# A windowed attention and two gated layers on one core: another order of the first loads, a fourth place for raw weights and for an attention unit, and filler products ahead of the first real one

## Chip, core and metric

The kernel runs on one core of a Trainium2 chip. The metric is the device time of one execution in microseconds (us). Three runs of the kernel before gave 659.75, 659.79 and 660.41 us, median 659.79.

## What is computed

```python
# attention, q, k, v: [2, 8, 768, 64]; a key is kept if it is one of the first 8 or at most 95 positions back
scores = scale * q @ k.T + bias(head, distance);  a = softmax(where(keep, scores, -1e9));  x = a @ v
x = x.transpose(0, 2, 1, 3).reshape(1536, 512)
y = ((x @ w_a) * (x @ w_b)) @ w_out            # d_ff 1536
h = y @ w_in                                   # d_ff 2048
g = where(h >= 1, h, where(h <= -1, 0, (h + 1)**2 / 4));  out = g @ w_out2
```

The weights come in double precision: the kernel gets each as 64 raw bits and makes two float32 halves (high and low) of it on the chip. Each of the large products is then three products: high by high, high by low and low by high.

## The kernel before

The 1536 rows are three tiles of 512. There are 24 **attention units** (tile, pair of heads, 256 rows). A unit's steps are: **scores** (S, L681 to L699), a minimum over the row with the mask added (VectorE, L711), the exponential with its sum (ScalarE, L723), an addition to the four sums (ScalarE, L731), a reciprocal (VectorE, L734), four **norms** (VectorE or GpSimd, L750), two **turns** (T, transposes on TensorE, L758, and their copies out of PSUM on ScalarE or VectorE, L764), and **values** (V, L775). The values' result is split into the two halves of x (L656, L657). In the first tile units alternate between a first block of rows (three 128-wide places, so T has 3+3 transposes and V is short) and a full one (4+4).

The **products** (p below, L459 and L487, the first four groups in L609) are 2460 matmuls of 128x512 in a fixed order; the first needs tile 0's first x and the first unit of weights. A unit of **weights** is 512 KB of raw bits (tile `raw`), loaded by `load_raw` into one of `NRAW` places and turned into two halves by seven steps (`prep`, L363 to L398: ScalarE L391, VectorE L392 to L395, a copy L402/L404, a subtraction L397). There are 68 such units.

All loads go out on SyncE's queue (SP). `Loads.begin` (L281) writes out the first ones before the branch on the flag; later ones are issued as places come free. The program uses eight load counters in turn, so each load also waits until the load eight before it has landed.

The order of everything after the branch is written by a planner at build time (`Clock`, L108): it keeps a model clock, sends an operation to the engine that would end it first by the durations given in the code, and advances by a given time for each step on TensorE. In the main loop (L995) it takes an attention step if one is due, or if the next product cannot start; otherwise a product. The chip then runs each engine's list in that fixed order, with waits on semaphores. So a wrong duration costs nothing by itself: it puts an operation at a place in an engine's list where it stands and waits while others behind it could go.

Of the kernel before, what the change touches and what calls it, by code (L numbers as in the profile page):

```python
# [10 lines left out]
F32 = mybir.dt.float32  # L11
F32R = mybir.dt.float32r
BF16 = mybir.dt.bfloat16
# [29 lines left out]

NRAW = 3

WARM = 10

TINY, HUGE = 3.0517578125e-05, 122880.0
# [10 lines left out]
HOP = dict(tensor=200, scalar=160, vector=170, gpsimd=120)  # L59
DMA = dict(issue=475, begin=1125, rate=360, end=900)  # L60

BEFORE = 4450

# [134 lines left out]
class Loads:  # L198
# [82 lines left out]
    def begin(self):  # L281
        self.load(0)
        self.load_raw(0)
        self.load(1)
        self.load_raw(1)
        self.load_v(0)
        self.load_raw(2)
        self.load(2)
        for n in range(3, NRAW):
            self.load_raw(n)  # L290
        self.load_v(1)

# [8 lines left out]
class Ffn:  # L301
    NW, MORE = 12, 2
    NM, MORE_M = 5, 4

    def __init__(self, ctx, tc, clock, loads, out, half):
        self.tc, self.nc, self.clock, self.loads, self.out, self.half = tc, tc.nc, clock, loads, out, half
        pool = lambda name, bufs, **kw: ctx.enter_context(tc.tile_pool(name=name, bufs=bufs, **kw))
        self.slots = []
        self.more_slots(ctx, "w_hl", self.NW)
        self.p_bits = pool("w_bits", 2)  # L310
        self.p_x = pool("x_hl", NP * NT)
        self.p_part = pool("part", NP * NT)
        self.mids = []
        self.more_mids(ctx, "mid", self.NM)
        self.p_s = pool("scr", 2)
        self.ps_acc = pool("ps_acc", 2, space=PSUM)
        self.ps_ab = pool("ps_ab", 2, space=PSUM)
        self.todo, units = plan()
        self.unit_no = {u: n for n, u in enumerate(units)}
        self.n_units = len(units)  # L320
        self.first_use, self.last_use = {}, {}
        for n, item in enumerate(self.todo):
            for u in units_of(item):
                self.first_use.setdefault(self.unit_no[u], n)
# [7 lines left out]
        self.in_flight = 0  # L332
        self.gap = GAP["first"]
        self.room = dict(ab=2, acc=2, s1=2, s2=2)
        clock.poll = self.prepare
# [27 lines left out]
    def prep(self, urgent):  # L363
# [11 lines left out]
        def chain(*steps):  # L375
            (emit, costs), rest = steps[0], steps[1:]

            def then():
                if len(rest) == 2:
                    self.loads.load_raw(u + NRAW, clock)  # L380
                if rest:
                    chain(*rest)
                else:
                    self.w[u] = wh, wl
                    self.in_flight -= 1

            clock.on(slack, emit, then, **costs)
# [200 lines left out]
    def early(self):  # L588
        nc = self.nc
        pools = [(self.ps_ab, "ab")] * 2 + [(self.ps_acc, "acc")] * 2  # L590
        pools = pools[: 2 * EARLY]
        early_ps = []
        for pool, tag in pools:
            self.take(tag)
            early_ps.append(pool.tile([P, T], F32, tag=tag, name=f"e{len(early_ps)}"))
        for c in range(NP):
            for n in range(2 * EARLY):
# [3 lines left out]
                yield lambda: u in self.w and (kind, t, c) in self.ready  # L601
                wh, wl = (a[:, c * P : (c + 1) * P] for a in self.w[u])
                xh, xl = self.x[0][c]
                ps = early_ps[n]
# [19 lines left out]
class Attention:  # L624
# [20 lines left out]
    def to_x(self, ps, t, p, col, w):  # L645
# [11 lines left out]
        lo = lambda e: e.tensor_tensor(places[1], ps[:, :w], as_f32(places[0]), ALU.subtract)  # L657
        low = lambda: clock.on(SLACK["x"], lo, then, None, False, vector=315)
        clock.on(SLACK["x"], hi, low, None, False, scalar=264, vector=315)


class Window(Attention):
# [4 lines left out]

    UNITS = 3

# [11 lines left out]
    def scores(self, st):  # L681
# [15 lines left out]
        w0, w1 = (w for _, w in places)  # L697
        ns = (w0 + w1) * 5 // 3 + w1 * 5 // 6 + 200
        self.write(ns, lambda: [self.reduce(st, j, r, ps[j]) for j in range(2) for r in range(NQ)])  # L699

    def reduce(self, st, j, r, ps):
# [14 lines left out]
        def reduced():  # L716
            st["read", j] = st.get(("read", j), 0) + 1
            if st["read", j] == NQ:
                self.give(ps)
            clock.on(SLACK["exp"], exp, share, scalar=100 + w * 25 // 16)  # L720

# [3 lines left out]
        def share():  # L725
            st["exp"] = st.get("exp", 0) + 1
            if st["exp"] == 2 * NQ:
                clock.on(SLACK["share"], add, lambda: clock.on(SLACK["share"], inverse, norms, None, False, vector=85), scalar=200)

# [6 lines left out]
        def norms():  # L736
            for jj in range(2):
                for rr in range(NQ):
                    clock.on(SLACK["norm"], *self.norm(st, jj, rr), gpsimd=457, vector=202)

        clock.on(SLACK["reduce"], least, reduced, lambda: not i or not self.masks.left, False, vector=w * 4 // 3)

# [9 lines left out]
    def turn(self, st, j):  # L752
# [11 lines left out]
        copy = lambda e: self.ffn.copy(e, pt[:, :n], ps[:, :n])  # L764
        self.write(n * 110 // P, lambda: clock.on(SLACK["turn"], copy, out, None, False, scalar=52 + n * 5 // 6, vector=n * 7 // 6))

    def values(self, st):

        ps, v = self.take(), st["v"]
        for r, (at, w) in enumerate(self.places(st)):  # L770
            parts = (0, 1) if w == self.W else (1,)
            for n, x in enumerate(parts):
                for j in range(2):
# [4 lines left out]
                    )  # L778
        ns = 1076 if st["i0"] else 807
        self.write(ns, lambda: self.to_x(ps, st["t_no"], st["p"], st["col"], NQ * P))  # L780

    def steps(self):
# [6 lines left out]
        def score(n):  # L789
            self.scores(units[n])  # L790
            loads.load(n + 3, self.clock)
            if n + 1 < len(units):
                nxt = units[n + 1]
                here = lambda: nxt.update(qs=True)
                scale = lambda e: loads.scale(e, n + 1, self.scales)
                self.clock.on(SLACK["qk"], scale, here, lambda: "here" in nxt, gpsimd=430, vector=200)

# [25 lines left out]
class Dense(Attention):  # L823


    def __init__(self, ctx, early, tc, clock, ffn, args, ident, ng, nl):
        super().__init__(ctx, tc, clock, ffn, ident)
        self.qz, self.k2, self.qd, self.kd, self.vd = args
        self.ng, self.nl = ng, nl
# [25 lines left out]
    def block(self, t, m):  # L855
# [5 lines left out]
        for p in range(NP):  # L861
            name = f"{b}_{i}_{p}"
            q = pool.tile([P, 2, P], F32, tag="q", name="q" + name)
# [3 lines left out]
            v = pool.tile([P, NB, 2 * D], F32, tag="v", name="v" + name)  # L867
            nc.sync.dma_start(v, self.vd[b, p, :, :, 1])
            nc.vector.tensor_scalar_mul(q, q, D**-0.5)
            po = self.ffn.ps_acc.tile([P, T], F32, tag="acc", name="o" + name)  # L870
            for j in range(2):
# [33 lines left out]
                for kb in range(NB):  # L905
                    nc.tensor.matmul(
                        po[row, :P], v[:, kb, row], st_[:, kb * P : (kb + 1) * P],
                        start=kb == 0, stop=kb == NB - 1,
# [15 lines left out]
def tile_kernel(ctx: ExitStack, tc: tile.TileContext, nn, qz, k2, qd, kd, vd, wu, out):  # L924
# [54 lines left out]
    with tc.If(near != 0, preferred_fallthrough_block=True) as cmp:  # L979
        with ExitStack() as arm:  # L980
# [14 lines left out]
            while holds:  # L995
# [8 lines left out]
                elif holds():  # L1004
                    passed += 1
                    holds = next(products, None)
                    if ffn.now == starts[2] and early:
# [3 lines left out]
                        ffn.more_mids(arm, "mid_more", ffn.MORE_M)  # L1011
                        ffn.gap = GAP["later"]
                else:
                    clock.turn()
            clock.drain()
    with cmp.Else():
        with ExitStack() as arm:
# [4 lines left out]
            early = arm.enter_context(ExitStack())  # L1022
            Dense(arm, early, tc, clock, ffn, (qz, k2, qd, kd, vd), ident, ng, nl).run()
            early.close()
# [110 lines left out]
```

## Time and profile before

| | |
|---|---|
| median of three runs | 659.79 us |
| the profiled execution | 660.28 us, span 658.5 us |
| TensorE (PE) busy | 643.0 us (98%), 3190 matmuls |
| VectorE (DVE) busy | 476.5 us (72%) |
| ScalarE (ACT) busy | 234.8 us (36%) |
| GpSimd (POOL) busy | 28.3 us (4%) |
| mean granted clock of PE | 0.991 of full |

Busy time of PE overlaps the tail of one matmul with the next, so that a busy PE may still be slower than it can be: single matmuls spread out read as busy. What one step costs when nothing holds it back is read from the chain of waits, where steps stand end to end.

### The profile page before, as it was taken

The page shows a single profiled execution, that of the slowest core. Times are in us where ns is not written, and L with a number is a line of the kernel's source. Part 1 is how long each engine was busy: PE and PEld are TensorE (multiplying, and loading weights), DVE is VectorE, ACT ScalarE, POOL GpSimd, SP SyncE. Part 2 cuts the span into 40 slices and gives each one's busy share as a digit, 9 for nine tenths or more (in the row PEclk, how much of TensorE's full clock was granted, in tenths as well). Part 3 has the DMA queues.
Part 4 walks back from the last instruction along what each step waited for, and adds up shares of the span by engine and source line. Part 5 has one row for each costly group of instructions (what it writes and reads, how often), then busy time and mean ns, then how long its engine had stood idle before and what let it go on. Part 6 is the DMA issues. An engine that isn't in the chain of part 4 may idle for free.

```text
span 658.5 us, 8812 instructions
## 1 busy us (share of the span) xinstructions
PE 643.0 (98%) x3190; PEld 514.4 (78%) x3190; DVE 476.5 (72%) x1071; ACT 234.8 (36%) x528; POOL 28.3 (4%) x64
## 2 busy tenths in 40 slices
PE   5999999999999999999999999999999999999997
PEld 2666677778888888888888888888888888888886
DVE  6999998537782837953848988785789688755552
ACT  4777775534241212311312323453334233311110
POOL 2223310000000000000000000000000000000000
PEclk7999999999999999999999999999999999999999
DMA  7666555101340211420212320321122111000112
GB/s 217 178 198 194 162 146 165 34 1 64 100 156 1 67 61 47 140 70 1 72 56 64 108 85 5 123 85 44 48 82 81 48 61 36 0 1 17 48 49 85
DMA packets 23763, 52.69 MB, mean 80 GB/s; under 512 B 3104, under 2 KB 11552, under 8 KB 23712
## 3 DMA queue, kind: packets, MB, share of 16 engines
q1 hardware_dynamic: 23568, 52.05, 25.4%
q8 instruction: 27, 0.44, 0.3%
q14 instruction: 24, 0.20, 0.1%
q10 hardware_dynamic: 144, 0.00, 0.0%
HBM read 48.89 MB, written 3.15 MB: 79 GB/s over the span
## 4 chain that ended last, share of the span: by engine, by line
PE 90%; DVE 5%; DMA 3%; SPq 1%; issue 1%; ACT 0%; DVEq 0%
PE ps L459 48%; PE o L487 20%; PE y L487 15%; PE at L775 2%; PE at L694 2%; PE at L758 2%; DVE p L711 1%; DMA v<-in_vd 1%; DMA k<-in_k 1%; DVE p L750 1%; PE e L609 1%; SPq L275 1%; DMA raw<-in_wu 1%; DVE bits L395 1%; DVE xlx L657 0%
## 5 line engine op out<-in xcount | busy, mean ns | idle before, releaser
L459 PE MATMUL ps<-xhx,w_hlh 128*128 128x512 f32 x224 | 88.7, 396 | 0.0
L459 PE MATMUL ps<-xlx,w_hlh 128*128 128x512 f32 x224 | 88.2, 394 | 0.0
L459 PE MATMUL ps<-xhx,w_hll 128*128 128x512 f32 x224 | 87.9, 392 | 0.0
L535 ACT ACTIVATE c<-c,half 128x512 f32<-128x512 f32 x48 | 34.7, 723 | 135.7 <-DVE c L532 135.7
L518 DVE TENSOR_TENSOR ab<-ps,a 128x512 f32<-128x512 f32 x34 | 23.4, 688 | 61.7 <-PE ps L459 61.4
L459 PE MATMUL ps<-xhy,w_hlh 128*128 128x512 f32 x168 | 65.4, 389 | 0.0
L459 PE MATMUL ps<-xly,w_hlh 128*128 128x512 f32 x168 | 65.4, 389 | 0.0
L459 PE MATMUL ps<-xhy,w_hll 128*128 128x512 f32 x168 | 65.4, 389 | 0.0
L532 DVE TENSOR_SCALAR c<-ps 128x512 f32<-128x512 f32 x48 | 33.1, 690 | 39.5 <-PE ps L459 39.4
L540 DVE TENSOR_TENSOR g<-ps,c 128x512 f32<-128x512 f32 x48 | 33.1, 690 | 24.2 <-ACT c L535 23.8
L402 ACT COPY a<-ps 128x512 f32<-128x512 f32 x28 | 16.4, 587 | 95.5 <-PE ps L459 91.7
L459 PEld LDWEIGHTS ps<-xhx,w_hlh 128*128 128x128 f32 x224 | 42.1, 188 | 9.3 <-issue 1.4
L391 ACT ACTIVATE bits<-raw 128x512 f32<-128x512 f32 x68 | 44.5, 667 | 13.4 <-DVE w_hll L397 6.1
L459 PEld LDWEIGHTS ps<-xlx,w_hlh 128*128 128x128 f32 x224 | 42.1, 188 | 9.2 <-issue 1.2
L459 PEld LDWEIGHTS ps<-xhx,w_hll 128*128 128x128 f32 x224 | 42.1, 188 | 9.0 <-issue 0.7
L395 DVE SCALAR_TENSOR_TENSOR bits<-raw,bits 128x512 uint32<-128x512 uint32 x68 | 46.4, 689 | 0.5
L394 DVE SCALAR_TENSOR_TENSOR bits<-raw,bits 128x512 uint32<-128x512 uint32 x68 | 46.1, 686 | 0.3
L402 ACT CAST w_hlh<-bits 128x512 fp32r<-128x512 f32 x46 | 28.4, 620 | 48.0 <-DVE bits L395 47.9
L397 DVE TENSOR_TENSOR w_hll<-bits,w_hlh 128x512 fp32r<-128x512 f32 x54 | 36.9, 685 | 1.7
L487 PE MATMUL y<-midh,w_hll 128*128 128x512 f32 x96 | 37.9, 394 | 0.0
L487 PE MATMUL y<-midh,w_hlh 128*128 128x512 f32 x96 | 37.8, 394 | 0.0
L487 PE MATMUL y<-midl,w_hlh 128*128 128x512 f32 x96 | 37.7, 392 | 0.0
(296 smaller groups left out, 1343.6 us busy)
## 6 DMA issues: line engine op xcount, KB each, us to landing
raw<-in_wu SPq DMA_DIRECT2D x68, 512.0 KB, 3.6
v<-in_vd SPq DMA_DIRECT2D x16, 256.0 KB, 4.1
k<-in_k SPq DMA_DIRECT2D x16, 200.0 KB, 3.6
q<-in_qd SPq DMA_DIRECT2D x48, 64.0 KB, 3.7
out<-opart SPq DMA_DIRECT2D x11, 256.0 KB, 2.0
k<-in_k SPq DMA_DIRECT2D x8, 128.0 KB, 3.3
v<-in_vd SPq DMA_DIRECT2D x8, 128.0 KB, 3.7
v<-in_vd SPq DMA_DIRECT2D x8, 64.0 KB, 3.8
```

Source lines behind the costliest of these rows:

```text
L391: (lambda e: e.activation(as_f32(b), as_f32(high), AF.Abs), dict(scalar=520)),
L394: (lambda e: e.scalar_tensor_tensor(b, low, 29, b, shr, or_), dict(vector=602)),
L395: (lambda e: e.scalar_tensor_tensor(b, high, 0xC0000000, b, both, or_), dict(vector=602)),
L397: (lambda e: e.tensor_tensor(wl, as_f32(b), as_f32(wh), ALU.subtract), SUB),
L402: e.copy(dst, src)
L459: nc.tensor.matmul(ps, l, r, start=c == 0 and m == 0, stop=last)
L487: nc.tensor.matmul(ps[:, cols], l, r[:, cols], start=f == lo and m == 0, stop=last)
L518: e.tensor_tensor(ab[0], ps, self.a.pop((t, f)), ALU.mult)
L532: e.tensor_scalar(c[0], ps, -1.0, 1.0, ALU.max, ALU.min)
L535: e.activation(c[0], c[0], AF.Square, bias=self.half, scale=0.5)
L540: e.tensor_tensor(g[0], ps, c[0], ALU.max)
L694: nc.tensor.matmul(ps[j][:, at : at + w], q[half, r * P : (r + 1) * P], k[half, k0 : k0 + w], start=True, stop=True)
```

## The change

The first loads come in another order, unit 1's q and k and unit 2's ahead of weights: q, k of 0; q, k of 1; raw 0; v 0; q, k of 2; raw 1; v 1; raw 2; raw 3. There is a fourth `raw` place, a raw place is loaded again when its unit's seven steps are all done instead of when two are left, four attention units may be in flight instead of three, and there are eight instead of nine pairs of `mid` tiles in the later stage. Until the first product has begun, the loop puts a filler matmul (128x256, bf16 bits of the identity, into a bank that is not yet used) wherever the model clock sees nothing for 107 ns. The model's durations and load times are other numbers (two of some fifteen lines are shown). The other arm of the branch takes its q and v tiles from the loads' places, which frees the room.

```diff
-NRAW = 3
+NRAW = 4
+FILL = 107
-DMA = dict(issue=475, begin=1125, rate=360, end=900)
-
-BEFORE = 4450
+DMA = dict(issue=580, begin=1600, rate=260, end=900)
+
+BEFORE = 5450
...
     def begin(self):
         self.load(0)
+        self.load(1)
         self.load_raw(0)
-        self.load(1)
+        self.load_v(0)
+        self.load(2)
         self.load_raw(1)
-        self.load_v(0)
+        self.load_v(1)
         self.load_raw(2)
-        self.load(2)
         for n in range(3, NRAW):
             self.load_raw(n)
-        self.load_v(1)
...
-    NM, MORE_M = 5, 4
+    NM, MORE_M = 5, 3
...
             def then():
-                if len(rest) == 2:
-                    self.loads.load_raw(u + NRAW, clock)
                 if rest:
                     chain(*rest)
                 else:
+                    self.loads.load_raw(u + NRAW, clock)
                     self.w[u] = wh, wl
...
-    UNITS = 3
+    UNITS = 4
...
-                    clock.on(SLACK["norm"], *self.norm(st, jj, rr), gpsimd=457, vector=202)
+                    clock.on(SLACK["norm"], *self.norm(st, jj, rr), gpsimd=457, vector=262 if self.places(st)[rr][1] > P else 198)
...
+                elif not ffn.begun and clock.events[0][0] >= clock.now + FILL:
+
+                    bits = ident.bitcast(BF16)
+                    nc.tensor.matmul(ffn.early_ps[-1][:, : 2 * P], bits[:, :P], bits, start=True, stop=True)
+                    clock.advance(FILL)
                 else:
                     clock.turn()
```

The lists that come of it differ at three places that matter below. SP's first loads before, from the first q to the branch (q_67, k_74 are unit 0's, q_68, k_75 unit 1's, q_69, k_76 unit 2's; raw_61 to raw_63 the first three units of weights):

```order
1 L275 DMA q_67<-in_qd 64x256 x2
2 L275 DMA k_74<-in_k 128x256
3 L275 DMA raw_61<-in_wu 128x1024
4 L275 DMA q_68<-in_qd 64x256 x2
5 L275 DMA k_75<-in_k 128x400
6 L275 DMA raw_62<-in_wu 128x1024
7 L275 DMA v_81<-in_vd 128x128
8 L275 DMA v_81<-in_vd 128x256
9 L275 DMA raw_63<-in_wu 128x1024
10 L275 DMA q_69<-in_qd 64x256 x2
11 L275 DMA k_76<-in_k 128x256
12 L275 DMA v_82<-in_vd 128x512
```

and now (every number one higher, so q_69, k_76 are unit 1's and raw_64 is the fourth place; unit 0's loads stand ahead as before, unit 3's follow behind the branch):

```order
3 L277 DMA q_69<-in_qd 64x256 x2
4 L277 DMA k_76<-in_k 128x400
5 L277 DMA raw_61<-in_wu 128x1024
6 L277 DMA v_82<-in_vd 128x128
7 L277 DMA v_82<-in_vd 128x256
8 L277 DMA q_70<-in_qd 64x256 x2
9 L277 DMA k_77<-in_k 128x256
10 L277 DMA raw_62<-in_wu 128x1024
11 L277 DMA v_83<-in_vd 128x512
12 L277 DMA raw_63<-in_wu 128x1024
13 L277 DMA raw_64<-in_wu 128x1024
```

Units 1 and 2 moved ahead of raw 0 and raw 1; raw 2 and a new raw 3 now stand ahead of unit 3.

VectorE's list before, from the reciprocal of unit 0 (st_0_0) to that of unit 1 (st_2_0):

```order
44 L734 RECIPROCAL st_0_0__270<-st_0_0__270 128x4
45 L395 SCALAR_TENSOR_TENSOR bits_281<-raw_61,bits_281 128x512
46 L256 TENSOR_SCALAR q_69<-q_69,scales 128x256
47 L392 TENSOR_SCALAR bits_303<-bits_303 128x512
48 L750 TENSOR_SCALAR p_0_0_0_271<-p_0_0_0_271,st_0_0__270 128x128
49 L750 TENSOR_SCALAR p_0_0_0_271<-p_0_0_0_271,st_0_0__270 128x256
50 L750 TENSOR_SCALAR p_0_0_1_272<-p_0_0_1_272,st_0_0__270 128x128
51 L750 TENSOR_SCALAR p_0_0_1_272<-p_0_0_1_272,st_0_0__270 128x256
52 L393 TENSOR_SCALAR bits_303<-bits_303 128x512
53 L734 RECIPROCAL st_2_0__292<-st_2_0__292 128x4
```

and now:

```order
42 L737 RECIPROCAL st_0_0__272<-st_0_0__272 128x4
43 L753 TENSOR_SCALAR p_0_0_0_273<-p_0_0_0_273,st_0_0__272 128x128
44 L753 TENSOR_SCALAR p_0_0_0_273<-p_0_0_0_273,st_0_0__272 128x256
45 L258 TENSOR_SCALAR q_70<-q_70,scales 128x256
46 L753 TENSOR_SCALAR p_0_0_1_274<-p_0_0_1_274,st_0_0__272 128x128
47 L753 TENSOR_SCALAR p_0_0_1_274<-p_0_0_1_274,st_0_0__272 128x256
48 L406 COPY p_0_0_0_273<-at_258 128x384
49 L394 TENSOR_SCALAR bits_309<-bits_309 128x512
50 L737 RECIPROCAL st_2_0__290<-st_2_0__290 128x4
```

The weight steps (bits) and the scaling of unit 2's q no longer stand ahead of unit 0's first norms; before the first of these rows the list of before also has three weight steps (L392 to L394) that the new one has not.

TensorE's list now, around the first turns (e_271<-ident is a filler, p_0_0_0 unit 0's first turn, k_77 unit 2's scores):

```order
53 L1021 LDWEIGHTS ident
54 L1021 MATMUL e_271<-ident 128x256
55 L761 MATMUL at_258<-ident,p_0_0_0_273 128x128 x3
56 L697 MATMUL at_259<-k_77,q_70 128x128
57 L697 MATMUL at_260<-k_77,q_70 128x128
58 L697 MATMUL at_259<-k_77,q_70 128x256
59 L697 MATMUL at_260<-k_77,q_70 128x256
60 L761 MATMUL at_261<-ident,p_0_0_1_274 128x128 x3
61 L1021 LDWEIGHTS ident
```

and before (k_76 is unit 2's there):

```order
31 L694 MATMUL at_256<-k_76,q_69 128x128
32 L694 MATMUL at_257<-k_76,q_69 128x128
33 L694 MATMUL at_256<-k_76,q_69 128x256
34 L694 MATMUL at_257<-k_76,q_69 128x256
35 L758 MATMUL at_258<-ident,p_0_0_0_271 128x128 x3
36 L758 MATMUL at_259<-ident,p_0_0_1_272 128x128 x3
37 L775 MATMUL at_256<-p_0_0_0_271,v_81 64x128
```

Unit 0's first turn now stands ahead of unit 2's scores. There are 23 fillers: 2 between the scores of units 0 and 1, 10 behind those of unit 1, 4 ahead of the values of unit 0, 3 ahead of those of unit 1 and 4 ahead of the scores of unit 3. Ahead of the first product stand three values steps before, two now.

## Rows read from the trace of the kernel before

**Rows 1.** Busy time by stretch: start:end, length, then engines, PEclk, DMA share, GB/s.
```profile
0.00:5.00 5.00, 3.81 (x9) 1.35 (x10) 2.78 (x16) 1.49 (x2) 2.46 (x22) 1.00 0.45 113
5.00:10.00 5.00, 2.70 (x16) 1.68 (x16) 3.47 (x19) 2.51 (x9) 0.48 (x1) 0.88 0.99 295
10.00:15.00 5.00, 1.61 (x11) 0.92 (x10) 3.75 (x16) 3.75 (x14) 0.00 (x0) 0.50 0.87 251
15.00:20.00 5.00, 4.93 (x30) 3.37 (x27) 3.98 (x17) 3.16 (x13) 1.54 (x3) 0.59 0.85 253
```

**Rows 2.** The same view, longer stretches (engines in the order PE, PEld, DVE, ACT, POOL).
```profile
20.00:40.00 20.00, 18.27 (x140) 11.97 (x137) 19.79 (x78) 14.66 (x50) 6.22 (x11) 1.00 0.60 168
80.00:97.00 17.00, 16.82 (x117) 11.86 (x116) 17.00 (x57) 11.95 (x39) 3.01 (x5) 1.00 0.49 147
97.00:145.00 48.00, 48.00 (x327) 35.36 (x326) 28.84 (x103) 26.07 (x79) 2.00 (x4) 1.00 0.23 71
200.00:400.00 200.00, 200.00 (x884) 165.61 (x883) 135.44 (x244) 47.37 (x78) 0.00 (x0) 1.00 0.21 64
```

**Rows 3.** Timeline of PE, 5 to 28 us: start, length, instruction, [idle before <- releaser].
```profile
5.62 0.93 PE L694 MATMUL at<-k,q 64*128 64x128 f32 x8
8.81 2.08 PE L694 MATMUL at<-k,q 64*128 64x256 f32 x8 [2.26 <-DMA k<-in_k]
14.28 1.65 PE L694 MATMUL at<-k,q 64*128 64x128 f32 x8 [3.39 <-DMA k<-in_k]
15.86 1.54 PE L758 MATMUL at<-ident,p 128*128 128x128 f32 x6
17.33 2.09 PE L775 MATMUL at<-p,v 128*64 128x128 f32 x12
...
26.47 0.88 PE L775 MATMUL at<-p,v 128*64 128x128 f32 x12
27.27 0.51 PE L609 MATMUL e<-xhx,w_hlh 128*128 128x512 f32 x1
```

**Rows 4.** Timeline of VectorE and ScalarE in the same stretch.
```profile
7.59 0.62 DVE L392 TENSOR_SCALAR bits<-bits 128x512 f32<-128x512 f32 x1 [0.94 <-ACT bits L391]
...
10.49 0.66 ACT L391 ACTIVATE bits<-raw 128x512 f32<-128x512 f32 x1 [0.18 <-SPq L1131]
...
13.76 0.35 DVE L256 TENSOR_SCALAR q<-q,scales 128x256 f32<-128x256 f32 x1 [0.75 <-SPq L1131]
14.03 0.42 DVE L392 TENSOR_SCALAR bits<-bits 128x512 f32<-128x512 f32 x1
14.37 1.00 DVE L750 TENSOR_SCALAR p<-p,st__270 128x128 f32<-128x128 f32 x4
```

**Rows 5.** Chain of waits, in order of time: start, length, what.
```profile
8.04 6.10 DMA k<-in_k
...
33.83 0.86 PE at L694 x8
34.68 0.81 PE at L775 x12
...
46.53 0.60 DVE p L404
...
47.46 0.60 DVE bits L394
48.06 0.34 DVE bits L393
...
73.81 0.34 PE at L758 x3
```

**Rows 6.** The same chain, later.
```profile
91.22 0.44 PE at L758 x4
...
99.30 1.02 PE at L775 x16
...
101.68 1.06 PE at L694 x8
```

More of the change, by code (lines that the diff above doesn't have):

```diff
@@ L332, in __init__ @@
         self.in_flight = 0
+        self.early_ps, self.begun = [], False
         self.gap = GAP["first"]
@@ L591, in early @@
         pools = pools[: 2 * EARLY]
-        early_ps = []
+        early_ps = self.early_ps
         for pool, tag in pools:
@@ L602, in early @@
                 wh, wl = (a[:, c * P : (c + 1) * P] for a in self.w[u])
+                self.begun = True
                 xh, xl = self.x[0][c]
@@ L657, in to_x @@
         lo = lambda e: e.tensor_tensor(places[1], ps[:, :w], as_f32(places[0]), ALU.subtract)
-        low = lambda: clock.on(SLACK["x"], lo, then, None, False, vector=315)
-        clock.on(SLACK["x"], hi, low, None, False, scalar=264, vector=315)
+        low = lambda: clock.on(SLACK["x"], lo, then, None, False, vector=334)
+        clock.on(SLACK["x"], hi, low, None, False, scalar=264, vector=334)
 class Window(Attention):
-    UNITS = 3
+    UNITS = 4
     def __init__(self, ctx, early, tc, clock, ffn, loads, ident, masks, scales):
@@ L697, in scores @@
         w0, w1 = (w for _, w in places)
-        ns = (w0 + w1) * 5 // 3 + w1 * 5 // 6 + 200
+        ns = (w0 + w1) * 5 // 3 + 210
         self.write(ns, lambda: [self.reduce(st, j, r, ps[j]) for j in range(2) for r in range(NQ)])
@@ L719, in reduced @@
                 self.give(ps)
-            clock.on(SLACK["exp"], exp, share, scalar=100 + w * 25 // 16)
+            clock.on(SLACK["exp"], exp, share, scalar=500 if w > P else 392)
         def exp(e):
@@ L727, in share @@
             if st["exp"] == 2 * NQ:
-                clock.on(SLACK["share"], add, lambda: clock.on(SLACK["share"], inverse, norms, None, False, vector=85), scalar=200)
+                clock.on(SLACK["share"], add, lambda: clock.on(SLACK["share"], inverse, norms, None, False, vector=85), scalar=96)
         def add(e):
@@ L738, in norms @@
                 for rr in range(NQ):
-                    clock.on(SLACK["norm"], *self.norm(st, jj, rr), gpsimd=457, vector=202)
-        clock.on(SLACK["reduce"], least, reduced, lambda: not i or not self.masks.left, False, vector=w * 4 // 3)
+                    clock.on(SLACK["norm"], *self.norm(st, jj, rr), gpsimd=457, vector=262 if self.places(st)[rr][1] > P else 198)
+        clock.on(SLACK["reduce"], least, reduced, lambda: not i or not self.masks.left, False, vector=345 if w > P else 216)
     def norm(self, st, j, r):
@@ L764, in turn @@
         copy = lambda e: self.ffn.copy(e, pt[:, :n], ps[:, :n])
-        self.write(n * 110 // P, lambda: clock.on(SLACK["turn"], copy, out, None, False, scalar=52 + n * 5 // 6, vector=n * 7 // 6))
+        self.write(146 + 52 * n // P, lambda: clock.on(SLACK["turn"], copy, out, None, False, scalar=20 + n * 9 // 10, vector=n * 7 // 6))
     def values(self, st):
@@ L778, in values @@
                     )
-        ns = 1076 if st["i0"] else 807
+        ns = 1024 if st["i0"] else 805
         self.write(ns, lambda: self.to_x(ps, st["t_no"], st["p"], st["col"], NQ * P))
@@ L795, in score @@
                 scale = lambda e: loads.scale(e, n + 1, self.scales)
-                self.clock.on(SLACK["qk"], scale, here, lambda: "here" in nxt, gpsimd=430, vector=200)
+                self.clock.on(SLACK["qk"], scale, here, lambda: "here" in nxt, gpsimd=453, vector=267)
         def value(n):
@@ L823, with __init__ @@
 class Dense(Attention):
-    def __init__(self, ctx, early, tc, clock, ffn, args, ident, ng, nl):
+    def __init__(self, ctx, early, tc, clock, ffn, loads, args, ident, ng, nl):
         super().__init__(ctx, tc, clock, ffn, ident)
+        self.loads = loads
         self.qz, self.k2, self.qd, self.kd, self.vd = args
@@ L862, in block @@
             name = f"{b}_{i}_{p}"
-            q = pool.tile([P, 2, P], F32, tag="q", name="q" + name)
+            q = self.loads.place["q"][0].rearrange("p (j n) -> p j n", j=2)
             nc.sync.dma_start(q, self.qz[b, p, :, i])
@@ L866, in block @@
             nc.sync.dma_start(k, self.k2[b, p])
-            v = pool.tile([P, NB, 2 * D], F32, tag="v", name="v" + name)
-            nc.sync.dma_start(v, self.vd[b, p, :, :, 1])
+            v = [self.loads.place["v"][n].rearrange("p a x n -> p (a x) n") for n in range(2)]
+            for n in range(2):
+                nc.sync.dma_start(v[n][:, : NB // 2], self.vd[b, p, :, n * NB // 2 : (n + 1) * NB // 2, 1])
             nc.vector.tensor_scalar_mul(q, q, D**-0.5)
@@ L906, in block @@
                     nc.tensor.matmul(
[L907 removed]
+                        po[row, :P], v[kb * 2 // NB][:, kb % (NB // 2), row], st_[:, kb * P : (kb + 1) * P],
                         start=kb == 0, stop=kb == NB - 1,
@@ L1022, in tile_kernel @@
             early = arm.enter_context(ExitStack())
-            Dense(arm, early, tc, clock, ffn, (qz, k2, qd, kd, vd), ident, ng, nl).run()
+            Dense(arm, early, tc, clock, ffn, loads, (qz, k2, qd, kd, vd), ident, ng, nl).run()
             early.close()
```

## Prediction

> **What bounds the kernel now.** I read the table by stretches first. From 97 us on PE is busy in every microsecond and VectorE has room (28.8 of 48 us), and between 200 and 400 us 884 matmuls take 200.0 us, 0.226 us each, with nothing between them [rows 2]. A gain can only come from before that, by letting PE reach this stretch earlier. From 20 to 97 us VectorE is busy all the time (19.8 of 20, 17.0 of 17) and PE nearly so [rows 2]. Before 20 us neither is: PE is busy 1.6 of 5 us between 10 and 15, and its granted clock falls to 0.50 there [rows 1].
>
> The timeline of PE then shows what it waited for: unit 1's k (2.26 us) and unit 2's k (3.39 us) [rows 3]. The first product starts only at 27.27 us. VectorE and ScalarE stand in front of loads too: VectorE waits for the raw bits' first step at 7.59 before it reduces unit 0's scores, and for unit 2's q at 13.76, with unit 0's norms queued behind it until 14.37; ScalarE gets to raw 1 at 10.49, with the addition that unit 0's reciprocal needs queued behind it [rows 4].
>
> **How much of the start is lost.** The chain, where steps stand end to end, gives what a step costs PE when nothing holds it: scores 0.86 us (first block) or 1.06 (full), a turn 0.34 or 0.44, values 0.81 or 1.02 [rows 5, 6]. When V of unit 2 ends (26.47 + 0.88 = 27.35 us, rows 3) PE has done five scores (3 x 0.86 + 2 x 1.06 = 4.70), six turns (4 x 0.34 + 2 x 0.44 = 2.24) and three values (2 x 0.81 + 1.02 = 2.64): 9.58 us of work in 27.35. So 17.8 us are lost, 5.6 of them before the branch [rows 3], which the change does not touch.
>
> **Term A, the start.** I walk the new lists with durations from the same rows. Bytes moved are 565 KB by 5 us, 2040 by 10, 3295 by 15 (113 x 5, + 295 x 5, + 251 x 5, rows 1). Raw 1 of before ends at 1608 KB of the queue, so 8.5 us, and is used at 10.49 [rows 4]; unit 2's k ends at 2568 KB, so 12.1 us, and is used 6.10 us after its issue at 8.04 [rows 5]. I take 2.0 us from the last byte to use.
> - Unit 1's q and k are now the next loads after unit 0's. Their bytes (584 KB) are there by 5.1 us; the issues, one in 0.6 us, make it 7.4. Scores of unit 1 at 7.4 to 8.5 (before 8.81 to 10.89).
> - VectorE has no weight step in front of unit 0's minima: 7.0 to 8.1. ScalarE's four exponentials take 1.9, and only one of unit 1's stands before the addition: the reciprocal at 10.0, the first two norms 10.5 (before 14.37).
> - Unit 2's q and k end at 1544 KB, 8.3 us, usable 10.6. First turn 10.8, scores of unit 2 at 11.1 to 12.0 (before 14.28), second turn 12.4.
> - ScalarE still has the first weight steps of raw 0 and raw 1 before the copy of that second turn; raw 1 now ends at 2056 KB, usable 12.1. The copy ends at 13.3, V of unit 0 starts at 13.35 (before 17.33).
> - T of unit 1 14.2 to 15.1 after its norms on GpSimd; its copies stand behind unit 2's exponentials on ScalarE and end at 16.3; V of unit 1 16.4 to 17.4.
> - VectorE has unit 3's q scaled at 19.3, behind two weight steps; scores 19.4 to 20.5. First weights done: first product at 20.5 (before 27.27), the scores of unit 4 by 21.9, one more product, V of unit 2 at 22.2 to 23.0, where unit 2's v, issued behind the loads of units 3 to 5, is the last to come.
>
> By 23.0 us PE has then done the same steps and three products more, 9.58 + 0.68 = 10.26 us of work: 12.7 lost instead of 17.8. **Term A is -5.0 us.**
>
> The walk assumes the full clock. Before, the clock was at 0.50 from 10 us on [rows 1] after a stretch with little work, and unit 0's values took 2.09 us there against 0.81 later [rows 3, 5]. In my walk PE's longest stop is 1.4 us, with fillers in the others. The Trainium skill ("TensorE: Matmul & The Clock Gate", Part 1: The HAM clock gate) says that the gate has two levels, falls after an idle stretch and rises again with work; the fall in rows 1 agrees. It speaks against the fillers as far as they stand where a model saw a gap, not where PE really waits; what a fall would cost is a rival below.
>
> **Term B, 23 to 97 us.** Here VectorE bounds as much as PE. Up to the low half of x of unit 17, about where PE alone becomes the bound, both kernels run the same 101 products and the same units. VectorE's list is lighter there: two copies of 384, one of 512, two of x's high half, one mid copy, three steps of one unit of weights and eight norms fewer, five q scalings and two subtractions more. At 0.47, 0.60, 0.34, 0.34, 1.54 (0.34 + 2 x 0.60), 0.25 (a quarter of the 1.00 of four norms), 0.27 (13.76 to 14.03) and 0.60 (the 0.47 scaled from 512) [rows 4, 5] that is -0.94 - 0.60 - 0.68 - 0.34 - 1.54 - 2.00 + 1.35 + 1.20 = -3.5 us. ScalarE and GpSimd take it over; ScalarE is at 14.7 of 20 us [rows 2], so it has room. VectorE also loses less at the start: it idles 3.8 us of the 15 from 5 to 20 us (15 - 3.47 - 3.75 - 3.98, rows 1) and in my walk some 0.5, so it could be 3.5 + 3.3 = 6.8 us earlier in all. Against it stands PE's own order: by V of unit 8 it has run 9 products instead of 23, so it does mostly attention, whose chain runs through VectorE, and may starve: 14 x 0.226 = 3.2 us. The ends are -1.8 (6.8 - 5.0) and +3.2; I take 0, since by V of unit 12 the products are level again (52 against 50) and VectorE, with 0.8 us less work to there, is still 4 us ahead.
>
> **Term C, the fillers.** 23 of 107 ns by the code's figure, 2.5 us if all delayed something. Each group stands ahead of a step that in my walk waits for VectorE or ScalarE; I take +0.2, ends 0 and 2.5.
>
> **The rest.** The fourth raw place, and reloading it two steps later, cost nothing after 97 us, where VectorE is 40% idle. Eight mid pairs hold the four of the group being summed and the four being made, so nothing waits; if the last did, VectorE's room would hide it. The 2256 products behind the last values step, and the end, are the same.
>
> **Sum.** -5.0 + 0 + 0.2 = -4.8 us. The profiled execution took 660.28, 0.49 above the median of the runs shown; against that median 659.79 - 4.8 = **655.0 us**.
>
> **Rivals.**
> - *VectorE's relief comes through whole* (term B at -1.8): 653.2. For it: VectorE is the busy one to 97 us. Against: PE is busy 16.8 of 17 us between 80 and 97 [rows 2], so it soon bounds. Chance 0.17.
> - *The clock falls all the same* while PE stands before unit 0's turns and values: scores, turns and values up to unit 1 at half speed, as 1.65, 1.54 and 2.09 us in rows 3 against 0.86, 0.68 and 0.81: 2.9 us more, of which some 2.1 lie on the path (V of unit 1 waits for ScalarE anyhow): 657.1. Chance 0.16.
> - *Products starve PE* (term B at +3.2, fillers at 0.6): -1.2, 658.6. The measurement of this kernel tells 0.2%, 1.3 us. Chance 0.09.
> - *Slower: the loads behind the bits.* Units 3, 4 and 5 now stand behind raw 2 and raw 3, 1 MB, and VectorE's scalings of their q's stand ahead of everything else in its list. Unit 2's k took 6.10 us behind one such load [rows 5]; two more take 3.6 us at 285 KB/us (the mean of rows 1 from 5 to 10 is 295), so unit 3's k, issued at 12.1, would land at 21.8 and not 18.5, and its scores come 2.5 us late. If units 4 and 5, whose loads also wait for raw 1, raw 2 and raw 3 to land, are late by as much again each, 7.5 us are lost: 662.5. It decides from a second repetition on (4.8 us). Against it: the queue moves 250 to 295 KB/us throughout, and 3920 KB are through at 17.5. Chance 0.07. The Trainium skill ("DMA: Bandwidth & Descriptors", Queues, rings and completion order) says that each DMA engine consumes its descriptors in ring order; by that rule too the small loads wait for the bits ahead of them.
> - The change does what it says: the fillers and moved steps are in the lists. What is left, 0.51, is the forecast.
>
> **The numbers.** Forecast (-3 to -6.5) 0.51, VectorE's relief 0.17, clock 0.16: faster by over 0.2% 0.84. Starving 0.09: within 0.2%. Loads 0.07: slower. The range leaves out 2 in 10: the slower case, the starved case and the far end of the relief. 651.5 to 658.4.
>
> **What would show it.** In the changed profile: scores of unit 1 near 7.4 us and no wait of PE for a k over 1.5 us; the clock at full from 5 to 25 us; V of unit 0 near 13.4 and the first product near 20.5; VectorE's idle time from 23 us on near none; the last values step ending near 139.8 instead of 144.6, with the same 510 us behind it. Wrong would be: a k or q that VectorE stands for after 18 us (slower rival), a clock of 0.5 between 12 and 19 us, or PE idle by more than 3 us between 23 and 50.

## The result and the profile after

The changed kernel took **652.08 us** (median of four runs, 651.82 to 653.21) beside 660.1 us for the kernel before on the same chip: a ratio of 0.988, 95% interval 0.9863 to 0.9897. That is 8.0 us less, where 4.8 were forecast; it lies in the range, towards its fast end. The profiled execution took 652.27 us, its span 650.5 us (before 660.28 and 658.5).

The table by stretches of the changed kernel, to be held against [rows 1, 2]:

```profile
5.00:10.00 5.00, 4.71 (x30) 2.66 (x28) 3.92 (x25) 2.67 (x13) 0.00 (x0) 1.00 0.94 267
10.00:15.00 5.00, 4.06 (x34) 2.79 (x35) 4.94 (x24) 4.54 (x18) 0.94 (x2) 1.00 0.99 356
15.00:20.00 5.00, 4.37 (x42) 3.34 (x41) 5.00 (x15) 3.31 (x10) 0.00 (x0) 1.00 0.70 177
20.00:40.00 20.00, 18.57 (x158) 12.31 (x155) 19.94 (x86) 17.57 (x66) 7.84 (x14) 1.00 0.79 226
23.00:40.00 17.00, 15.57 (x137) 10.58 (x132) 16.94 (x70) 14.57 (x58) 6.10 (x12) 1.00 0.81 230
23.00:97.00 74.00, 71.91 (x558) 51.22 (x552) 71.72 (x256) 57.79 (x193) 19.41 (x36) 1.00 0.67 197
80.00:97.00 17.00, 17.00 (x118) 12.40 (x116) 15.95 (x46) 10.43 (x29) 2.17 (x5) 1.00 0.54 163
97.00:145.00 48.00, 48.00 (x310) 36.99 (x309) 23.97 (x88) 25.63 (x76) 2.25 (x4) 1.00 0.15 47
200.00:400.00 200.00, 200.00 (x884) 165.62 (x883) 140.17 (x255) 48.43 (x80) 0.00 (x0) 1.00 0.20 64
```

Between 10 and 15 us the granted clock is 1.00 instead of 0.50, and PE is busy 4.06 us instead of 1.61. From 23 to 97 us, the stretch of term B, VectorE is no longer busy in every microsecond: 71.72 of 74. The row of before for that stretch is

```profile
23.00:97.00 74.00, 70.33 (x529) 48.26 (x528) 74.00 (x267) 55.05 (x185) 21.87 (x34) 1.00 0.60 177
```

From 97 us on PE is always busy in both kernels, and 884 matmuls take 200 us as before. So nearly the whole gain has to arise ahead of that.

The timeline of PE in the changed kernel, 5 to 24 us (before: [rows 3]; L1021 is a filler, L697 scores, L761 turns, L778 values, L612 products):

```profile
7.20 0.39 PE L1021 MATMUL e<-ident 128*128 128x256 bf16 x2
7.52 1.14 PE L697 MATMUL at<-k,q 64*128 64x256 f32 x8
8.59 1.27 PE L1021 MATMUL e<-ident 128*128 128x256 bf16 x10
10.73 0.70 PE L761 MATMUL at<-ident,p 128*128 128x128 f32 x3 [0.88 <-DVE p L753]
11.36 0.93 PE L697 MATMUL at<-k,q 64*128 64x128 f32 x8
...
13.13 0.43 PE L778 MATMUL at<-p,v 128*64 128x128 f32 x2
...
16.00 1.66 PE L778 MATMUL at<-p,v 128*64 128x128 f32 x16
...
19.38 1.20 PE L697 MATMUL at<-k,q 64*128 64x256 f32 x8 [0.48 <-DVE q L258]
20.51 0.50 PE L612 MATMUL e<-xhx,w_hlh 128*128 128x512 f32 x1
...
22.46 0.88 PE L778 MATMUL at<-p,v 128*64 128x128 f32 x12
```

PE stands for no k any more; its longest waits here are for unit 0's norms (0.88 us) and for the scaling of unit 3's q (0.48 us). The norms that the walk put at 10.5 stand in VectorE's timeline at 10.39 (14.37 in [rows 4]):

```profile
10.39 0.55 DVE L753 TENSOR_SCALAR p<-p,st__272 128x128 f32<-128x128 f32 x2
```

The chain of waits tells the rest. In the kernel before, VectorE's last pieces on it, and the last values step, are

```profile
85.97 1.50 DVE p L750 x2
87.48 0.04 issue
87.52 0.44 PE at L758 x2
...
143.59 1.02 PE at L775 x16
144.62 13.85 PE ps L459 x60
```

and in the changed one

```profile
47.83 0.81 DVE w_hll L399
48.65 0.04 issue
48.69 2.34 PE e L612 x9
...
135.58 1.02 PE at L778 x16
136.60 13.83 PE ps L461 x60
```

Up to 87.5 us the chain still came back to VectorE; now it leaves it at 48.7 us and stays on PE to the end. The last values step ends at 136.6 instead of 144.6, and the 60 products behind it take the same time (13.83 and 13.85 us): all 8.0 us are there. At V of unit 17, which ends at 92.6 instead of 100.3, 7.7 of them are.

### The profile page after: what moved, and what is told of

The parts are those of the page before. It is cut to its first block, busy times and chain, and to the rows that moved or that the text cites. A ratio compares the mean times of both kernels' runs of the same rounds, so it can differ in the third digit from the quotient of the medians.

```text
span 650.5 us, 8868 instructions
## 1 busy us (share of the span) xinstructions
PE 640.5 (98%) x3213; PEld 514.9 (79%) x3213; DVE 469.1 (72%) x1058; ACT 238.7 (37%) x539; POOL 26.8 (4%) x66
## 4 chain that ended last, share of the span: by engine, by line
PE 93%; DVE 3%; issue 0%; ACT 0%
PE ps L461 49%; PE o L489 20%; PE y L489 15%; PE at L697 3%; PE at L778 3%; PE at L761 2%; PE e L612 2%; DVE p L714 1%; DVE p L753 1%; DVE xlx L660 0%; DVE p L406 0%; DVE bits L396 0%; DVE bits L397 0%; DVE w_hll L399 0%; DVE bits L395 0%
## 5 line engine op out<-in xcount | busy, mean ns | idle before, releaser
L404 ACT COPY a<-ps 128x512 f32<-128x512 f32 x27 | 15.9, 588 | 96.4 <-PE ps L461 92.6
L397 DVE SCALAR_TENSOR_TENSOR bits<-raw,bits 128x512 uint32<-128x512 uint32 x68 | 46.0, 685 | 0.5
L399 DVE TENSOR_TENSOR w_hll<-bits,w_hlh 128x512 fp32r<-128x512 f32 x58 | 39.8, 689 | 1.7
L489 PE MATMUL o<-w_hlh,midl 128*128 128x512 f32 (+1 forms) x101 | 39.1, 387 | 0.0
L489 PE MATMUL o<-w_hll,midh 128*128 128x512 f32 (+1 forms) x101 | 39.1, 387 | 0.0
L489 PE MATMUL o<-w_hlh,midh 128*128 128x512 f32 (+1 forms) x101 | 39.1, 387 | 0.0
```

The costliest lines, as they stand in the source:

```text
L397: (lambda e: e.scalar_tensor_tensor(b, high, 0xC0000000, b, both, or_), dict(vector=602)),
L399: (lambda e: e.tensor_tensor(wl, as_f32(b), as_f32(wh), ALU.subtract), SUB),
L404: e.copy(dst, src)
L489: nc.tensor.matmul(ps[:, cols], l, r[:, cols], start=f == lo and m == 0, stop=last)
```

## Experiments

Times are medians, of four runs where no other number is given; each ratio is to the kernel before on the same chip (660.2 to 660.5 us), with its 95% interval. Where "the changed kernel" is compared, that is 652.08 us and 0.988, which were measured beside 660.1 us for the kernel before. Times inside a run (us from its start) are those of its one profiled execution.

**The fillers.**

```diff
-                    nc.tensor.matmul(ffn.early_ps[-1][:, : 2 * P], bits[:, :P], bits, start=True, stop=True)
```

> The changed kernel with every filler matmul left out and all other lists the same. Theory (the fillers hold TensorE's clock through the start): the granted clock falls to about 0.5 somewhere between 10 and 20 us, values of unit 0 and the steps around it take up to twice as long, first product some 2 us later than 20.5, and the time is about 654.2, 2.1 us over the changed kernel. Rival (the attention steps, now closer together, hold the clock by themselves, so the fillers only stand in the way): clock at full, time 651.8 to 652.1.

653.50 us, 0.9896 (0.9877 to 0.9914); the profiled execution took 654.33. All lists are the same but for the 23 fillers. By stretches, then on PE:

```profile
5.00:10.00 5.00, 3.12 (x18) 1.65 (x16) 4.10 (x26) 2.71 (x13) 0.00 (x0) 1.00 0.97 261
10.00:15.00 5.00, 4.37 (x20) 2.63 (x22) 4.25 (x20) 3.80 (x14) 0.93 (x2) 0.53 1.00 377
15.00:20.00 5.00, 4.63 (x39) 3.65 (x36) 3.98 (x13) 2.81 (x10) 0.00 (x0) 0.78 0.65 164
```

```profile
11.51 1.65 PE L697 MATMUL at<-k,q 64*128 64x128 f32 x8
...
13.93 2.18 PE L778 MATMUL at<-p,v 128*64 128x128 f32 x12
...
22.36 0.50 PE L612 MATMUL e<-xhx,w_hlh 128*128 128x512 f32 x1
```

After a stretch in which PE was busy 3.12 of 5 us instead of 4.71, the clock is 0.53 on the mean of the next, near the lower of its two levels (1.2 GHz), and the steps there take longer: scores of unit 2 1.65 us instead of 0.93, values of unit 0 2.18 instead of 1.5 with a wait in them. The first product comes at 22.36 instead of 20.51, V of unit 2 ends 1.9 us later, and the last values step 1.8 us later (138.4): what the start loses is lost to the end. The fillers are worth 1.4 us by the medians, 2.1 by the profiles, and delay nothing that shows.

**The order of the first loads**, put back in the changed kernel and put alone into the kernel before:

```diff
         self.load(0)
-        self.load(1)
         self.load_raw(0)
-        self.load_v(0)
-        self.load(2)
+        self.load(1)
         self.load_raw(1)
-        self.load_v(1)
+        self.load_v(0)
         self.load_raw(2)
+        self.load(2)
...
+        self.load_v(1)
```

> The changed kernel with the first loads in the order of before (the fourth raw place behind unit 2). Theory (the 4.7 us that the start gained come mostly from unit 1 and unit 2 no longer standing behind bits): scores of unit 1 at 8.8 and of unit 2 near 14 us again, values of unit 2 near 25 to 26 instead of 22.5, time about 655. Rival (the planner's durations and load times bring the start, since a list that fits the real landing times stands nowhere): scores as late, but the first product within 1 us of 20.5 and the time under 653.

652.93 us, 0.9889 (0.9872 to 0.9905): 0.9 us lost, less than the intervals can tell from nothing. Unit 1's k comes at 9.40, V of unit 2 ends at 26.8 instead of 23.3. But the first product starts at 21.32, only 0.8 us later than in the changed kernel: the planner, with its new load times, expected the k's late and had put other steps there, and six products instead of three stand ahead of V of unit 2.

> The kernel before with the changed order of first loads alone, three raw places, old planner times. Theory A (the order of loads by itself is worth little, as the changed kernel with the old order took 652.93): 659 to 660. Rival (in a list that was made for wrong landing times the earlier q and k are worth the 4.7 us of the start): about 656.

658.25 us, 0.9976 (0.9965 to 0.9987; eight runs): 1.9 us gained (2.9 in the profiled execution, which was the fastest of the eight). V of unit 2 ends at 22.05 instead of 27.34, earlier than in the changed kernel:

```profile
21.18 0.88 PE L775 MATMUL at<-p,v 128*64 128x128 f32 x12
```

The first product follows at 21.98 instead of 27.27. But V of unit 3 ends at 31.7, only 1.6 us ahead of before, the clock is 0.90 from 23 to 40 us, VectorE stays busy 20.00 of 20 us from 40 to 60 and from 60 to 80, and of the 5.3 us only 2.9 are left at the last values step (141.7).

**The durations of attention steps in the planner**, put back in the changed kernel (two of ten lines shown; load times stay new):

```diff
-            clock.on(SLACK["exp"], exp, share, scalar=500 if w > P else 392)
+            clock.on(SLACK["exp"], exp, share, scalar=100 + w * 25 // 16)
...
-        clock.on(SLACK["reduce"], least, reduced, lambda: not i or not self.masks.left, False, vector=345 if w > P else 216)
+        clock.on(SLACK["reduce"], least, reduced, lambda: not i or not self.masks.left, False, vector=w * 4 // 3)
```

> The changed kernel with the durations of attention steps in the planner as before; load times of the planner, load order, places and fillers as changed. Theory A (the second part of the gain, 3.4 us after 23 us, comes from lists that fit the chip: VectorE gets less, ScalarE and GpSimd more): start the same, VectorE without idle time from 23 to 97 us, last values step near 139.5, time about 655. Rival B (it comes from the start alone, or from four units in flight): time within 0.7 us of 652.1.

657.34 us, 0.9954 (0.9938 to 0.9971). No other single edit costs as much: 5.3 of the 8 us. Some of it is the clock: the two runs with a mean clock of 0.999 took 656.6 and 656.7 us, the two with 0.995 and 0.996 took 658.0. Its stretch of term B, and its clock at the start, where the fillers now stand at the wrong places:

```profile
10.00:15.00 5.00, 3.40 (x16) 2.38 (x16) 4.24 (x20) 3.24 (x12) 0.94 (x2) 0.66 1.01 375
23.00:97.00 74.00, 71.35 (x535) 49.88 (x535) 74.00 (x273) 56.39 (x187) 14.53 (x22) 1.00 0.61 177
```

VectorE is saturated again from 23 to 97 us, as before, and GpSimd is used for 14.5 us where the changed kernel uses it for 19.4. V of unit 2 ends at 24.5 (1.2 us later), the last values step at 142.1 (5.5 later): some 4 us of the loss arise behind the start. The chain of waits comes back to VectorE and, behind it, ScalarE until 91.6 us, as it did to VectorE until 87.5 in the kernel before:

```profile
86.10 0.60 DVE p L753 x2
...
87.08 2.08 ACT p L726 x8
```

> The kernel before with the changed planner's durations and load times alone; loads, places, units in flight as before, no fillers. Theory A (lists that fit the chip bring most of the gain): VectorE has idle time between 40 and 97 us, first product some us before 27.3, time 654 to 656. Rival (it takes the new loads, the fourth unit and the fillers): over 658.5.

All of the planner's new times (durations and loads) alone in the kernel before: 657.75 us, 0.9963 (0.9949 to 0.9978). 2.4 us gained, between the two expectations. VectorE gets room from 60 us on (19.02 of 20), but the clock is 0.50 from 10 to 20 us, where the kernel before was at 0.50 and 0.59, so the start of this run doesn't show what the lists would do at the full clock.

> The kernel before with the new order of first loads and the changed planner's durations and load times together; three raw places, three units in flight, no fillers. If the two add up as each alone (1.9 and 2.4 us of 660.2), 655.9. Theory A (they belong together: loads that come early are only used by lists that count on them): 654 to 655, with VectorE idle between 40 and 97 us. Rival (what one brings the other brings too): 657 to 658.

Both together: 655.94 us, 0.9934 (0.9912 to 0.9955), 4.3 us gained. The two parts add up (1.9 + 2.4) as far as an interval of 1.4 us to either side can tell, and 3.7 of the 8 us are left for fillers, fourth unit, fourth raw place and the rest.

**The fourth unit.**

```diff
-    UNITS = 4
+    UNITS = 3
```

> The changed kernel with three attention units in flight as before, all else as changed. Theory A (lists that fit the chip bring the second part): within 0.7 us of 652.1. Rival B (the fourth unit gives TensorE attention steps to do while products wait for weights): TensorE idle between 25 and 60 us, time about 655.

655.49 us, 0.9934 (0.9918 to 0.9951): 3.4 us lost; 2.8 in the two runs with a mean clock of 0.999 (654.79 and 654.91), while the other two had 0.996 and 0.994. From 23 to 40 us PE is busy 14.61 of 17 us instead of 15.57:

```profile
23.00:40.00 17.00, 14.61 (x126) 9.64 (x122) 17.00 (x68) 13.82 (x54) 5.50 (x11) 1.00 0.82 242
```

One wait is longer than that whole difference. PE stands 1.63 us for a norm; the norm stands on VectorE behind a weight step that takes 1.76 us instead of 0.69, beside a subtraction on GpSimd:

```profile
37.51 0.90 PE L761 MATMUL at<-ident,p 128*128 128x128 f32 x5 [1.63 <-DVE p L753]
35.10 1.76 DVE L396 SCALAR_TENSOR_TENSOR bits<-raw,bits 128x512 uint32<-128x512 uint32 x1
37.12 0.80 DVE L753 TENSOR_SCALAR p<-p,st__570 128x256 f32<-128x256 f32 x3
35.04 1.27 POOL L399 TENSOR_TENSOR w_hll<-bits,w_hlh 128x512 fp32r<-128x512 f32 x1
```

In the changed kernel GpSimd makes no subtraction between 22 and 62 us. So this run shows what the list with three units ran into, and not that PE lacks steps with three units as such. The last values step ends 1.5 us later (138.1). In the profiled execution another 1.0 us lies behind the last matmul (646.82 to 653.0, against 645.34 to 650.5). From the end of the last matmul to the end of the span it is 4.8 to 5.9 us in the fourteen profiles, 5.9 here, so this need not come from the units; it was not traced.

**The fourth raw place and the time of reloading.**

```diff
-NRAW = 4
+NRAW = 3
```

> The changed kernel with three raw places, so without raw 3 among the first loads; all else as changed. If the fourth place lets weights be ready in time (products would otherwise wait for bits while attention runs ahead): 1 to 3 us slower, 653 to 655. Rival (it only holds bits that wait anyhow): within 0.7 us of 652.1.

653.37 us, 0.9895 (0.9878 to 0.9911): 1.3 us lost. PE, which waits for nothing behind 97 us in the changed kernel, stops for 1.2 us there:

```profile
97.00:145.00 48.00, 46.80 (x304) 34.96 (x303) 26.41 (x88) 24.02 (x71) 4.28 (x7) 1.00 0.20 61
```

The stop is two waits at 106 to 108 us, 0.57 us for norms on GpSimd and 0.62 for the scaling of a q on VectorE. Neither is for weights, so the size expected came and the reason given for it is not shown.

> The changed kernel with the room of the fourth raw place given to a fifth attention unit in flight. If units in flight are what TensorE lacks (the fourth brought 3.4 us): faster than with three raw places and four units by 1 us or more. Rival (four cover the chain of one unit, and the products then wait for weights): the same as with three raw places and four units, or slower.

Five units with three raw places: 652.08 us, 0.9874 (0.9857 to 0.989). With a fifth unit the median is 1.3 us below that with four, though the intervals overlap, and it is no better than the changed kernel.

The reload of a raw place, back at two steps left:

```diff
+                if len(rest) == 2:
+                    self.loads.load_raw(u + NRAW, clock)
...
-                    self.loads.load_raw(u + NRAW, clock)
```

> The changed kernel, but a raw place is loaded again when two of its unit's seven steps are left, as before. If raw places bound the weights: up to 1.5 us faster, 650.5 to 652. Rival (loads that come earlier stand ahead of q, k and v on the queue, or nothing waits for them): within 0.7 us of 652.1 or up to 1 us slower.

652.51 us, 0.9884 (0.9868 to 0.9901): no difference that can be told. With four places the time of the reload makes no difference of more than the noise.

**What VectorE is worth**, at unchanged lists: lighter in the kernel before, heavier in the changed one.

```diff
-            (lambda e: e.tensor_scalar(as_f32(b), as_f32(b), HUGE, TINY, ALU.min, ALU.max), CLAMP),
-            (lambda e: e.tensor_scalar(b, b, 3, 0x3FFFFFF8, shl, both), dict(vector=335)),
+            (lambda e: e.tensor_scalar(as_f32(b)[:, :cut], as_f32(b)[:, :cut], HUGE, TINY, ALU.min, ALU.max), CLAMP),
+            (lambda e: e.tensor_scalar(b[:, :cut], b[:, :cut], 3, 0x3FFFFFF8, shl, both), dict(vector=335)),
```

> The kernel before with all lists the same, but the two steps L392 and L393 of the first eleven units of weights done on 64 of 512 columns, which takes some 0.24 us off each of 22 VectorE instructions, 5.2 us in all (the clamp, shift and mask are left out for the other columns). Theory A (VectorE bounds the stretch from 20 to 97 us): 3 to 4.5 us faster, 655.5 to 657. Rival B (TensorE's own order, with its switches between attention and products, bounds it): less than 1 us faster.

656.92 us, 0.9953 (0.9937 to 0.997): about 5.2 us less work on VectorE takes 3.2 us off the kernel before. The last values step ends at 140.9 instead of 144.6; 1.2 of these 3.7 us are there at V of unit 2 (26.12 instead of 27.34), where the clock from 15 to 20 us was 0.81 instead of 0.59, and 2.5 come behind it. So VectorE did bound that stretch.

```diff
-            (lambda e: e.tensor_scalar(b, b, 3, 0x3FFFFFF8, shl, both), dict(vector=335)),
+            (lambda e: [e.tensor_scalar(b, b, 3, 0x3FFFFFF8, shl, both) for _ in range(2 if u < 11 else 1)], dict(vector=335)),
```

> The changed kernel with all lists the same, but step L395 of the first eleven units of weights written twice, 0.34 us more on VectorE each, 3.7 us in all (the weights get a second shift). Theory A (VectorE bounded before, and the change gave it room: 2.2 us of idle time from 23 to 97 us): between 1 and 2.5 us slower, 653 to 654.6. Rival (VectorE still bounds): 3.4 us slower, 655.5. Rival B (it never did): within 0.5 us of 652.1.

654.43 us, 0.9915 (0.9898 to 0.9931): 3.7 us more work on VectorE cost the changed kernel 2.3. So VectorE still has a hold on it, mostly in the part ahead of 48 us where the chain runs through it: of the 2.0 us that the last values step is later, 1.6 are there at V of unit 8 (48.68 instead of 47.11).

## Why the prediction was right, and where it was too small

The time lies in the range, but not in the main case (3 to 6.5 us less, chance 0.51): one of the two large terms came as said, the other did not.

**Term A held.** The walk said, and the trace shows: scores of unit 1 at 7.4 (7.52), first turn 10.8 (10.73), scores of unit 2 at 11.1 (11.36), V of unit 0 at 13.35 (13.13), V of unit 1 at 16.4 (16.00), scores of unit 3 at 19.4 (19.38), first product 20.5 (20.51), end of V of unit 2 at 23.0 (22.46 + 0.88 = 23.34). PE had lost 23.34 - 10.26 = 13.1 us by then instead of 17.8: -4.7 us where -5.0 was said. Two sizes carried it: 2.0 us from a load's last byte to its use, and the cost of steps from the chain.

**What term A stood on was half the matter.** The prediction put it on the loads. How much PE had lost at the end of a values step (the time less the work done by then at the prediction's prices, a product at 0.226) tells what each part did:

| us lost by PE at the end of V of unit | 2 | 3 | 17 |
|---|---|---|---|
| kernel before | 17.8 | 19.1 | 29.3 |
| kernel before with the new order of loads | 13.3 | 18.3 | 26.4 |
| kernel before with the planner's new times | 17.0 | 18.4 | 25.4 |
| kernel before with both | 13.7 | 16.6 | 24.6 |
| changed kernel | 13.1 | 14.7 | 21.6 |
| changed kernel with the old order of loads | 14.8 | 16.2 | 22.6 |
| changed kernel with the old durations | 14.3 | 17.2 | 26.8 |

The new order of loads alone brings 4.4 of the 4.7 us by V of unit 2, so there the prediction was right. But in a list made for other times 3.6 of these are gone again one unit later, though that run's clock, 0.90 from 23 to 40 us, has a part in it. Only with the new times is more of it kept. In the changed kernel the old order costs 1.7 us at V of unit 2 and 0.9 in the end, since the planner then fills the waits with products; the fillers (1.4 us) keep the clock up beside it.

**The step that failed is term B**, "I take 0". At V of unit 17, up to which both kernels have run the same 101 products, PE is 100.3 - 92.6 = 7.7 us ahead; 4.7 of these it had at V of unit 2. Term B measured -3.0 us (another 0.3 comes by V of unit 23). That is past the end of the bounds (-1.8), on the side of the rival "VectorE's relief comes through whole" (chance 0.17), and more than it was priced at. Three things were wrong in the step:

- *The starving was expected to eat the relief.* PE's waits from 23 to 97 us are 74 - 71.91 = 2.1 us; before they were 3.7. Between V of unit 2 and V of unit 8, up to which PE runs 14 products fewer, it lost 18.1 - 13.1 = 5.0 us instead of 24.2 - 17.8 = 6.4. So nothing starved. The prediction gave the fourth unit no term at all; taken out, it costs 3.4 us, of which the profile shows 1.1 at V of unit 17.
- *"PE soon bounds, so VectorE's relief ends there" was no objection.* VectorE left the chain at 48.7 us instead of 87.5. As long as it was there, the lightening counted: 3.2 us of 5.2 in the kernel before, by the experiment.
- *VectorE's list was priced by instructions at their usual length.* Some took far longer before, in places that the sum of counts doesn't see. Up to V of unit 17 VectorE makes eight of the low halves of weights (the subtraction, L399) instead of six (L397), as the prediction counted, and GpSimd two instead of six. VectorE was charged for the two taken over, and nothing was credited for what those on GpSimd had done to it. VectorE's busy time from 5 us to the end of V of unit 17 (third column of engines), before and now:

```profile
5.00:100.33 95.33, 85.90 (x631) 58.74 (x629) 91.17 (x330) 68.25 (x225) 23.89 (x38) 0.95 0.64 190
```

```profile
5.00:92.56 87.56, 83.61 (x654) 58.89 (x652) 84.52 (x319) 69.49 (x231) 21.61 (x39) 1.00 0.71 208
```

That is 6.7 us less, where the count gave 3.5. VectorE, then GpSimd, in the kernel before at two of the six subtractions:

```profile
50.09 2.23 DVE L750 TENSOR_SCALAR p<-p,st__654 128x256 f32<-128x256 f32 x3
...
85.90 1.57 DVE L750 TENSOR_SCALAR p<-p,st__1098 128x128 f32<-128x128 f32 x2
```

```profile
50.15 1.28 POOL L397 TENSOR_TENSOR w_hll<-bits,w_hlh 128x512 fp32r<-128x512 f32 x1
...
86.04 1.28 POOL L397 TENSOR_TENSOR w_hll<-bits,w_hlh 128x512 fp32r<-128x512 f32 x1
```

Three norms take 2.23 us instead of about 1.0 (3 x 0.34 on the chain), two take 1.57 instead of about 0.6, each time beside a subtraction on GpSimd; a weight step at 24.11 us takes 0.99 instead of 0.43 and one at 68.44 takes 1.12 instead of 0.69 in the same way. Together that is 1.2 + 1.0 + 0.6 + 0.4 = 3.2 us of VectorE. Counting every VectorE instruction up to V of unit 17 that runs more than 0.15 us past the median of its kind, all of them beside some GpSimd step, it is 4.9 us. Of its two subtractions the changed kernel shows one such place, a weight step at 63.02 of 0.72 instead of 0.43, and 0.7 us in all. The second of the groups above is VectorE's last piece on the chain of the kernel before (1.50 us from 85.97), and with three units PE stood 1.63 us behind another. That this is the missing part is read from the traces; no run moved the subtractions alone, so it is not shown. Such time does not simply add to the kernel's: the changed kernel with the old order of loads has 2.9 us of it and loses 0.9. The Trainium skill ("SBUF — State Buffer", SBUF: two separate sides) says that VectorE, for some of its operations, and GpSimd share one pair of ports that one instruction holds until it has ended, with the other waiting. The rows agree: the longest of the three norms took 1.48 us, and VectorE's minima, which read PSUM, ran at their usual 0.42 us (57.96) beside the subtraction of 56.97 to 58.26.

**The other steps.** Term C was +0.2; no delay by fillers shows, and what they give back was counted within A by the full clock it assumed. "The clock falls all the same" did not come: 1.00 throughout. Without the fillers it does fall, and the price given for it, 2.1 us, is what that profile shows. "Loads behind the bits" did not come: unit 3's scores waited 0.48 us for the scaling of its q and began when the walk had them, and no repetition followed. "The rest" was wrong in one part: the fourth raw place, put at nothing, is worth 1.3 us, though the reloading time is worth nothing that can be told. Of the signs named, two failed with term B: VectorE's idle time "near none" from 23 us on was 2.3 us up to 97, as PE became the bound earlier, and the last values step ended at 136.6 instead of 139.8.

**What stays open.** The parts taken out one at a time (5.3, 3.4, 1.4, 1.3 and 0.9) sum to 12.3 us, more than the whole; they act on the same waits, and their shares are not settled. Not tried were the subtractions on GpSimd moved alone, the planner's durations without its load times in the kernel before, fillers in the kernel before, and eight pairs of `mid` tiles alone. The longer end behind the last matmul with three units is not explained.

## What to carry to other kernels

Where engines run fixed lists that a planner wrote, measured durations in its model are an optimization of their own: here putting back ten lines of durations, which change no instruction but its place and engine, costs 5.3 of the 8 us. They are not worth as much by themselves: with the new load times alone they bring the kernel before 2.4 us. An earlier load is kept only by a list that counts on it. A relief of an engine that is busy all the time should be taken as worth most of its size (here 3.2 of 5.2 us, and 2.3 of 3.7 the other way) unless a row shows what else holds the next engine, and the relief includes instructions that run longer than usual because of a neighbour, so read the longest ones and not the mean alone. Where a start must wait for loads, filler matmuls in the gaps pay for themselves if the granted clock falls in the stretch behind.

## What the hardware showed that was not expected

- A subtraction of 1.28 us on GpSimd can hold VectorE's norms and weight steps up, a norm of 0.34 us to 1.48 us. Of the six before V of unit 17 in the kernel before four did, for 0.4 to 1.1 us each; on VectorE itself the operation takes 0.69 us.
- Without fillers the drop of the clock is not the same in every execution: two runs with a mean granted clock of 0.994 took 654.33 and 654.38 us, two with 0.997 and 0.998 took 652.68 and 652.66. The Trainium skill ("TensorE: Matmul & The Clock Gate", Part 1: The HAM clock gate) says that how many matmuls run slow at the start differs from run to run of one kernel; these four differ likewise, if behind a gap and not at the kernel's own start.
